# One order of steps for another: the merge of attention and MLP in seven of eight loops (RWKV-6 attention, then an exact-GELU MLP)

## The chip, the core and the metric

The kernel runs on one core of a Trainium2 chip. The metric is the device time of one execution in microseconds (us); lower is better.

## The reference

Attention is a linear recurrence over 768 positions, for 4 batches x 8 heads of 48 values; an MLP with the exact GELU follows on its output. All of it is fp32.

```python
for t in range(S):                       # S = 768
    kt, vt, rt, wt = (k[:, :, t], v[:, :, t], r[:, :, t], w[:, :, t])
    cur = np.einsum('bhd,bhe->bhde', u[None] * kt, vt)
    y[:, :, t] = np.einsum('bhd,bhde->bhe', rt, state + cur)
    state = wt[:, :, :, None] * state + np.einsum('bhd,bhe->bhde', kt, vt)
x = y.transpose(0, 2, 1, 3).reshape(3072, 384)
h = x @ w_in                             # 384 -> 2048
g = 0.5 * h * (1.0 + erf(h / sqrt(2)))
return g @ w_out                         # 2048 -> 384
```

## The kernel before

The 3072 tokens are cut into eight tiles of 384 (half a batch each). For each tile there are three generators of work, and a `yield` in them ends a *step*:

- `attention(x, unit)` works in chunks of 64 positions. DVE lays out the decayed r and k (L394, L401, L407, L427, L435, and L579 with ACT's L573 in `quarters`); PE multiplies them in small 64x64 matmuls, in bursts (`burst`, L595 and L604); DVE and ACT copy the results into the score tile `a_sb` (L637, L687 on DVE, L620 on ACT, where a later copy and the next burst on the same banks wait for each other). `blocks_of_k` transposes k on DVE (L552), and 12 DMAs on the SP queue (L547) move its blocks; L711 on ACT copies the rest (in the second tile PE's transposes L701 and ACT's L703 do this). Then come the matmuls into `kv_ps` (L727), a chain of 20 or so small DVE operations that carries the state from chunk to chunk (L742), the matmuls of scores by v into `y_ps` (L768, `inside`), two small DVE copies that read `y_ps` (L780, `fences`), and the matmuls of the state by r into the same `y_ps` (L813), which wait for the fences. ACT copies `y_ps` to `xT` (L836, L839), and DMAs move a part of it (L843).
- `mlp(x)` takes `xT`. *h passes* are the first product: L1070 for the first two tiles, L945 for the others (in halves, combined by sums so that fewer products are needed), with GELU on ACT (L1073, L1075, L977, L981). *o passes* are the second product: L1164 for the first tile, L1084 for the others, four or eight matmuls to a step; ACT and DVE take the results from PSUM (L1120 to L1207, among them L1181, L1203 and L1207 near the end of a tile).
- `load(x)` issues the DMAs of a tile's r, k, w and v on the SP queue (L192, L172). `sums_of_x` (L913 on DVE) prepares sums of `xT` for the MLP; it reads what the DMAs of L843 bring. In the second tile `w_sums` (L860) and in the third `first_sum` and `h_sums` make sums of the weights on DVE, and up to the second tile `conversion` turns fp64 weights into fp32 (L349, L350, L352 on ACT, L361 and L365 on DVE).

Loop `x` of eight merges the MLP of tile `x - 1`, the attention of tile `x`, the head of the attention of tile `x + 1` and the loads of tile `x + 1`. The merge is written out by hand: `PLAN[x]` is a string, and each of its characters takes one step of a stream:

```python
for c in PLAN[x]:
    next(streams[c], None)
```

The letters are `.` for `mlp(x - 1)`, `s` for `attention(x)`, `f` for the head of `attention(x + 1)`, `l` for the loads, `x` for `sums_of_x`, `w` for masks and sums of weights, `c` for the conversion. (In loop 0 they stand for other streams.) What a string leaves over is taken behind it, stream by stream. Behind the last loop `mlp(7)` runs alone.

The schedule is manual: instructions go to each engine's queue in the order in which the steps issue them, and each engine works through its queue in that order, waiting by semaphores for what an instruction needs. So a string decides what stands ahead of each instruction on PE, ACT, DVE and on SP's queue of DMAs. Loops are called 0 to 7 here; loop 1 makes the attention of the second tile. On PE the loops begin at 48.9 (loop 1), 124.4, 197.1, 261.3, 332.5, 396.7 and 467.9 us (loop 7), and `mlp(7)` at 532.4 us of the profiled execution.

Of the kernel before, what the change touches and what calls it, by code (L numbers as in the profile page):

```python
# [38 lines left out]
PLAN = {  # L39
    0: ".lls.....sslsc.lsslll.sl.sls..sl.lscsl..sss.lscs.lscs.s.clll.s..s.pcsss...wss..sccs.ffp",  # L40
    1: (
        ".cswc.ccc.cccss.lc.ccscs..cc.cs.cclwcsc.ccssc.c.cccsccc..ssccc.c.lcls.cc.ccsc.w.clwscclccc"
        ".c.swcw.ss.ccs.lcsc..cwcccslccslff..w..fw.wfs..f..flffffffww"
    ),
    2: (
        "...l...s..ws.swssswssss.sslsw...ssss.sssws.ll..ws.w..lw.sw.wl.sls.sls..lf.s....sf..f.f.xx."
        "fxl.x.x"
    ),
    3: (
        "l..sss..s.s..s.s....s...s.ssllss.sss.s.s.ss.l..lsss..ssslss.ss.s..s......s..ls.llssf.sf.sf"  # L50
        "lf.f.x.x..xxfffxf"
    ),
    4: (
        "...s...lsl......s.s....sss..ssss..s..ss..s..s...llssslss....sl.sss...s...sll.sl.s.sfs..fsf"
        ".ff..xl.x.xfffxffx"
    ),
    5: (
        ".l..........ls.ss...s.sslls.ssss..ss.sls...sss..sssssl.ss.s..s.......s.lssll.sfsf.f.s.ff.x"
        "..x.xxxl"
    ),  # L60
    6: (
        "sss.sls.....s......ls.s....s.sssssss..s.....s.ss....s.s.ssss.s.l.ss.l.ls.l...s.l.lslssf.s."
        ".ffs..lff.xx..xffxffx"
    ),
    7: "......s.s....s.s...s.ssssss...sss.ss...sss..ssss.s...ss...s...s.s.ss.s.s.s.x.x...xxx",
}


# [5 lines left out]
def kernel(  # L74
# [6 lines left out]
    w_out: bass.AP,  # L81
    out: bass.AP,
):

    nc = tc.nc  # L100
    NX = rkw.shape[0]
    NP = u.shape[1]
# [1227 lines left out]
```

## Time and the profile before

| | |
|---|---|
| three runs, us | 593.58, 595.18, 594.47; median 594.47 |
| profiled execution, first to last instruction | 595.7 us (1.2 above the median; nothing further is shown around it) |
| instructions | 17417 |
| PE busy | 578.9 us, 97%, 7536 matmuls |
| DVE busy | 440.2 us, 74% |
| ACT busy | 280.9 us, 47% |
| POOL busy | 8.0 us, 1% |
| DMA | 46.80 MB, mean 79 GB/s |

PE is TensorE's matmuls, DVE is VectorE, ACT is ScalarE, POOL is GpSimd, SP is SyncE, whose queue issues the DMAs. In the profile's lines `out<-in` names the tiles; `xN` is a number of instructions; a bracket holds the idle time of the engine ahead of an instruction and what ended it. In the table by stages each line has the stretch and its length, then the busy time of PE, PEld (weight loads), DVE, ACT and POOL, the clock granted to PE (1.00 is full speed), the share of DMA and the GB/s.

### The profile page before, as it was taken

To read this page: it belongs to the slowest core of one execution; us is meant where nothing else is said; L and a number is where in the kernel's file an instruction comes from. 1 tells how busy PE (TensorE), PEld (TensorE's weight loads), DVE (VectorE), ACT (ScalarE), POOL (GpSimd) and SP (SyncE) were. 2 spreads that over 40 slices of the span, in tenths; PEclk is the share of its full clock that TensorE was granted. 3 is DMA by queue.
4 is the path that set the end of the run, shared out by engine and by line. 5 is a ranking of instruction groups with operands and counts; after the bars stand their busy time and mean duration, and the time that the engine had idled before them with its cause. 6 is when DMAs were issued, how large, how long until landed. Compare 5 with 4: busy or idle time off the path is not lost. (4 is left out here: it accounts for less than half of the span.)

```text
span 595.7 us, 17417 instructions
## 1 busy us (share of the span) xinstructions
PE 578.9 (97%) x7536; PEld 513.5 (86%) x7536; DVE 440.2 (74%) x854; ACT 280.9 (47%) x648; POOL 8.0 (1%) x21
## 2 busy tenths in 40 slices
PE   5789999999999999999999999999999999999998
PEld 3566666676799999999999999999999999999997
DVE  5868767888969987687859987688759998521332
ACT  2158889333622358045561458135560465435400
POOL 3100000000000000000000000000000000000000
PEclk9989999999999999999999999999999999999999
DMA  7657671120152211241023411330015200210000
GB/s 235 193 175 273 211 237 61 71 94 1 19 148 79 74 54 24 74 137 36 1 52 90 124 37 18 96 110 11 3 32 161 72 2 5 37 46 0 1 15 33
DMA packets 51004, 46.80 MB, mean 79 GB/s; under 512 B 31728, under 2 KB 36080, under 8 KB 50928
## 3 DMA queue, kind: packets, MB, share of 16 engines
q1 hardware_dynamic: 50832, 45.62, 25.5%
q8 instruction: 59, 0.97, 0.7%
q14 instruction: 17, 0.14, 0.1%
q10 hardware_dynamic: 96, 0.07, 0.1%
HBM read 36.24 MB, written 4.72 MB: 69 GB/s over the span
## 5 line engine op out<-in xcount | busy, mean ns | idle before, releaser
L945 PE MATMUL h_ps<-xT,w_in_sb 128*128 128x192 f32 x480 | 95.4, 330 | 0.5 <-DVE o_sb L1207 0.5
L945 PEld LDWEIGHTS h_ps<-xT,w_in_sb 128*128 128x128 f32 x480 | 79.7, 190 | 3.9 <-ACT g L977 1.5
L1070 PE MATMUL h_ps<-xT,w_in_sb 128*128 128x384 f32 x192 | 64.5, 491 | 0.9 <-ACT rkw L1075 0.9
L1070 PEld LDWEIGHTS h_ps<-xT,w_in_sb 128*128 128x128 f32 x192 | 35.7, 190 | 25.5 <-ACT rkw L1075 1.7
L1084 PE MATMUL o_ps<-w_out_sb,g 128*128 128x192 f32 x224 | 39.7, 326 | 0.0
L1084 PEld LDWEIGHTS o_ps<-w_out_sb,g 128*128 128x128 f32 x224 | 37.0, 190 | 0.3
L945 PE MATMUL u_ps<-s,w_in_sb 128*128 128x192 f32 x192 | 35.3, 327 | 0.0
L468 PEld LDWEIGHTS d<-rkw 64*64 64x64 f32 x1152 | 20.8, 147 | 16.7 <-issue 11.9
L620 ACT COPY a_sb<-d 32x256 f32<-32x256 f32 (+8 forms) x90 | 32.6, 362 | 4.6 <-PE d L604 3.1
L945 PEld LDWEIGHTS u_ps<-s,w_in_sb 128*128 128x128 f32 x192 | 31.8, 190 | 0.2
L1084 PE MATMUL o_ps<-w_out_sb,f 128*128 128x192 f32 x176 | 31.6, 329 | 0.0
L1084 PE MATMUL o_ps<-t,g 128*128 128x192 f32 x176 | 31.4, 329 | 0.0
L1084 PE MATMUL o_ps<-w_out_sb,e 128*128 128x192 f32 x176 | 31.4, 329 | 0.0
L1084 PE MATMUL o_ps<-t,e 128*128 128x192 f32 x176 | 31.2, 328 | 0.0
L1084 PE MATMUL o_ps<-t,s 128*128 128x192 f32 x176 | 30.9, 327 | 0.0
L468 PE MATMUL d<-rkw 64*64 64x64 f32 (+1 forms) x1152 | 23.5, 235 | 7.2 <-DMA rkw<-in_rkw_dram 4.1
L742 DVE SCALAR_TENSOR_TENSOR st<-st,tot_sb,kv_ps 128x48 f32<-128x48 f32 x160 | 29.0, 256 | 1.7 <-PE kv_ps L727 1.6
L637 DVE COPY_PREDICATED a_sb<-quarter,d 128x480 f32<-128x480 uint8 (+5 forms) x54 | 23.2, 438 | 8.6 <-PE d L604 7.3
L1084 PEld LDWEIGHTS o_ps<-t,g 128*128 128x128 f32 x176 | 28.7, 190 | 0.4
L1084 PEld LDWEIGHTS o_ps<-w_out_sb,e 128*128 128x128 f32 x176 | 28.7, 190 | 0.3
L1084 PEld LDWEIGHTS o_ps<-w_out_sb,f 128*128 128x128 f32 x176 | 28.7, 190 | 0.3
L1084 PEld LDWEIGHTS o_ps<-t,e 128*128 128x128 f32 x176 | 28.8, 190 | 0.2
(163 smaller groups left out, 1127.0 us busy)
## 6 DMA issues: line engine op xcount, KB each, us to landing
rkw<-in_rkw_dram SPq DMA_DIRECT2D x54, 256.0 KB, 4.0
raw<-in_w_out_dram SPq DMA_DIRECT2D x8, 768.0 KB, 4.5
v_in<-in_v_dram SPq DMA_DIRECT2D x8, 584.0 KB, 3.9
raw<-in_w_in_dram SPq DMA_DIRECT2D x5, 768.0 KB, 6.5
out_dram<-o_sb SPq DMA_DIRECT2D x20, 192.0 KB, 2.0
rkw<-kx SPq DMA_DIRECT2D x72, 48.0 KB, 2.0
rkw<-in_rkw_dram SPq DMA_DIRECT2D x6, 384.0 KB, 6.8
raw<-in_w_in_dram SPq DMA_DIRECT2D x9, 256.0 KB, 4.7
```

The lines of the kernel that those rows point to most:

```text
L468: nc.tensor.matmul(d[half[p], g, n * width:(n + 1) * width], lhsT=kc[half[g], b, i, p], rhs=right(half[g], b, i, p), start=True, stop=True)
L620: nc.scalar.copy(out=at[z, g, first:behind, (a + 1) * h:], in_=d[z, :, :, to] if g == slice(None) else d[z, :, to])
L637: nc.vector.copy_predicated(out=an[:, :, :, :, (a + 1) * h:], mask=mask.to_broadcast(data.shape), data=data)
L742: nc.vector.scalar_tensor_tensor(out=stq[:, q, c], in0=stq[:, q, c - 1] if c else b4[:, q, NC - 1], scalar=totq[:, q, c:c + 1], in1=kvs[q ...
L945: nc.tensor.matmul(o, lhsT=lhsT, rhs=rhs, start=start, stop=True, skip_group_check=True)
L1070: nc.tensor.matmul(h_ps, lhsT=w_in_sb[:, f // FI, j, f % FI * 128:(f % FI + 1) * 128], rhs=xT[:, j, :], start=(j == 0), stop=(j == NJ - 1))
L1084: nc.tensor.matmul(o, lhsT=lhs(j), rhs=rhs(j), start=start and j == 0, stop=(j == HF - 1), skip_group_check=True)
```

## The change

The strings of loops 1 to 7 are replaced by others with the same steps in another order. Within each stream the order of steps stays as it was; between the streams it changes. Where a string holds fewer `f` than before, those steps of the head come in the next loop, as `s`. The string of loop 0 stays, as does all code that issues instructions. Sixteen blank lines at the head of the kernel go, so that a line's number is 16 lower afterwards (L813 becomes L797).

```diff
 PLAN = {
     0: ".lls.....sslsc.lsslll.sl.sls..sl.lscsl..sss.lscs.lscs.s.clll.s..s.pcsss...wss..sccs.ffp",
     1: (
-        ".cswc.ccc.cccss.lc.ccscs..cc.cs.cclwcsc.ccssc.c.cccsccc..ssccc.c.lcls.cc.ccsc.w.clwscclccc"
-        ".c.swcw.ss.ccs.lcsc..cwcccslccslff..w..fw.wfs..f..flffffffww"
+        "c.c.s.cs.ccc.csccscs.c.ccc.cccslcccss.sc.cl.sccccccs..l.wwcsc.c.cscccc.cs.c..sscwlc.cc.ccl"
+        "cswsccwccsccwcw.cl.csl.sccllf..c.ff...w.sffswwfwlw...."
     ),
     2: (
-        "...l...s..ws.swssswssss.sslsw...ssss.sssws.ll..ws.w..lw.sw.wl.sls.sls..lf.s....sf..f.f.xx."
-        "fxl.x.x"
+        "s.l.sss.lss.s..ss.ss.wwws.ss.w.lw.ss.lsssss.s.wsss.sssw.w..l.w...l.sws..ls.sls..l...fsfl.."
+        "sf.f..fx.xxxx"
     ),
     3: (
-        "l..sss..s.s..s.s....s...s.ssllss.sss.s.s.ss.l..lsss..ssslss.ss.s..s......s..ls.llssf.sf.sf"
-        "lf.f.x.x..xxfffxf"
+        "sll.ss.sss....s....s....ss.ssss..s..ssss.l.l.s.sss..ssss.sss.l........s.ssl.s.slsllslsf.f."
+        ".f.fxxxxx...f"
     ),
     4: (
-        "...s...lsl......s.s....sss..ssss..s..ss..s..s...llssslss....sl.sss...s...sll.sl.s.sfs..fsf"
-        ".ff..xl.x.xfffxffx"
+        "ls..s..s.sl...sls...s..s...sl.sssss..s..ss.lss..s.....s.ssl..s.ss..ss.s....s.s.ls.ss.llfs."
+        "ff.s..ff.l.xx.xfxx"
     ),
     5: (
-        ".l..........ls.ss...s.sslls.ssss..ss.sls...sss..sssssl.ss.s..s.......s.lssll.sfsf.f.s.ff.x"
-        "..x.xxxl"
+        "sls.s..sl..l...ss....sl.l..s.ssss.s.sss..s.ss...sss.sssss..s..s..l..s..s.slssls..lsfs..f.x"
+        "f.x.fx.x.fxl"
     ),
     6: (
-        "sss.sls.....s......ls.s....s.sssssss..s.....s.ss....s.s.ssss.s.l.ss.l.ls.l...s.l.lslssf.s."
-        ".ffs..lff.xx..xffxffx"
+        "l.ss.sss........s..lls.s..l.l.ss.lss.ss..s.ss...ss..s..s..s..s.ssss..ss.s....ssl..ls.slfsf"
+        "..fs.ffx..x..xxxl"
     ),
-    7: "......s.s....s.s...s.ssssss...sss.ss...sss..ssss.s...ss...s...s.s.ss.s.s.s.x.x...xxx",
+    7: "ss..s..s.....ss.s..s...s.sssssss...ss...s..ssss.sssss..s....s..s.s...ssss...ss....xxx.xx",
 }
```

## The prediction

> **What bounds the kernel now.** I read the busy times of the page first, then the table by stages (one stretch per loop), the list of what PE waited for, and the chain that ended last. The page:
> ```profile
> PE 578.9 (97%) x7536; PEld 513.5 (86%) x7536; DVE 440.2 (74%) x854; ACT 280.9 (47%) x648; POOL 8.0 (1%) x21
> ```
> PE is busy for 578.9 of 595.7 us. The stages, cut at the loops' starts on PE (after the span come PE, PEld, DVE, ACT, POOL, clock, DMA share, GB/s):
> ```profile
> 48.00:124.00 76.00, 75.09 (x1072) 49.81 (x1071) 59.02 (x93) 58.98 (x98) 0.00 (x0) 1.00 0.50 165
> 124.00:197.00 73.00, 73.00 (x788) 58.07 (x786) 63.71 (x121) 24.65 (x63) 0.00 (x0) 1.00 0.23 67
> ...
> 332.00:396.00 64.00, 63.67 (x832) 60.67 (x832) 52.44 (x98) 32.28 (x84) 0.00 (x0) 1.00 0.25 67
> 396.00:468.00 72.00, 71.63 (x871) 69.18 (x870) 58.28 (x111) 33.01 (x83) 0.00 (x0) 1.00 0.23 65
> ```
> PE fills each loop that the change touches (75.1 of 76, 73 of 73, 63.7 of 64, 71.6 of 72 us), the clock is full, and DVE has 9 to 17 us to spare in each of these four. So the time there is PE's work plus PE's stalls, and an order changes only these. The stalls:
> ```profile
> PE d L468 <- DMA rkw<-in_rkw_dram: 4.1, 1, 4.1
> PE d L468 <- issue: 2.3, 2, 1.8
> PE h_ps L1070 <- ACT rkw L1075: 0.9, 1, 0.9
> PE y_ps L768 <- DVE st L742: 0.7, 2, 0.4
> PE h_ps L945 <- DVE o_sb L1207: 0.5, 1, 0.5
> ```
> The first two are in the first tile, whose order stays. In the loops of the second to the eighth tile I count, from row to row of PE's timeline (start to start, which finds a little more than the list): 1.04 us (57.53, L1070 behind L1075), some 0.28 us twice at kv_ps (242.8 and 314.1, behind the DMAs of L547), 0.17, 0.27, 0.50 and 0.53 us at y_ps (behind the chain of states, L742), and 0.71 us at 468.4 (L945 behind L1207); together 3.8 us. That is all which a better order of the same work could win by stalls. The chain shows the last of them:
> ```profile
> 467.95 0.35 DVE o_sb L1203
> 468.30 0.28 DVE s L913
> 468.61 0.36 DVE xT L913
> 468.96 0.28 DVE o_sb L1207
> 469.29 2.22 PE h_ps L945 x12
> 471.51 0.65 PE u_ps L945 x4
> 472.16 2.15 PE h_ps L945 x12
> 474.30 1.30 PE u_ps L945 x8
> 475.60 1.95 PE h_ps L945 x12
> ```
>
> **What the change can win.** No instruction comes or goes; the steps of the streams are merged otherwise. Twelve h passes take 1.95 us in a row, and 2.15 us where they follow attention's 64x64 matmuls (last fence): a visit to these costs 0.2 us. I count the visits from the two strings, with the steps that hold matmuls: 9, 6, 7, 6, 7, 6, 7 in loops 1 to 7 before, and 8, 6, 6, 6, 6, 6, 6 after. Four fewer save 0.8 us. With the 3.8 us of stalls the ceiling of any gain is 4.6 us (0.8%). Issues of DMAs move on SP too: the loads of the next tile (4.0 us to landing) are awaited by DVE alone (0.5 us at L407 in loop 3 of before), which has time to spare; I put them at 0, and at 1 us if that spare time is gone (in the upper bound). The other DMAs are costed below.
>
> **What it can lose.** For each matmul that needs ACT or DVE, I took from the timeline how long its producer had been done (its slack), and added up what stands ahead of both in the new order, with the mean of each row. Where PE's work ahead shrinks more than the slack, or the producer's queue gets longer by more, PE waits. Differences to before, by loop:
>
> Loop 1. kv_ps (L727) comes 1.4 us of PE earlier, while the same ACT work stands ahead of its copies (a conversion L349, L350, L352 of 2.9 us, then L529, and L703 at 0.80 each). Its slack was 0.26 us, so it waits 1.1; I take 0.9, as PE already stands 0.4 us later by two waits behind L1075 (+0.3 and +0.1: a conversion is now queued ahead of them on ACT). The y_ps wait of 0.17 goes. In the string the last two "s" were parted by "." and are now parted by "ff", which is DVE work alone: the matmuls of L813 stand right behind those of L768 on PE, with only the fence between. Its latency shows at loop 7 of before:
> ```profile
> 521.21 1.63 PE L768 MATMUL y_ps<-a_sb,v_in 64*64 64x64 f32 x96
> 522.91 0.16 DVE L780 COPY fence<-y_ps 128x2 f32<-128x2 f32 x1 [0.45 <-PE y_ps L768]
> 524.26 1.63 PE L813 MATMUL y_ps<-rkw,st 64*64 64x64 f32 x96
> ```
> PE's next row began at 522.83, and the fence ended at 523.07, behind an idle DVE: 0.3 us with the signal back, which the o pass in between covered. With no pass between, it costs 0.3 (more if DVE is late). One visit less: -0.2. Sum: 0.9 + 0.4 - 0.17 + 0.3 - 0.2 = +1.2 us.
>
> Loop 1 into 2. L1181 frees the bank that the second h pass of L1070 needs; it had 1.75 us to spare. Its "." now comes after "wwfwlw", and DVE has behind the fence two of L427's (1.0), two of L401's steps with one L435 (2.2 and 2.5), four of L860 (0.95 each) and L1181 itself:
> ```profile
> 124.26 0.36 DVE L1181 TENSOR_TENSOR o_sb<-o_ps,rkw 128x192 f32<-128x192 f32 x1 [1.49 <-issue]
> ```
> That is 1.0 + 2.2 + 2.5 + 3.8 + 0.36 = 9.9 us, against 9.2 us of PE from the fence to that pass (L813 1.6, four o passes 5.3, the two of L131 0.4, the first h pass 1.9): +0.6. In before the same DVE had been idle here (1.49 us, the bracket). Attention's first d burst (L604) then waits 0.2 for L579, and kv_ps 0 to 0.5 for the DMAs of L547, issued 5 us later; I take 0.2. Sum: +1.0.
>
> Loop 3. The first burst arrives 1.4 us earlier against a slack of 1.23: +0.25. The kv_ps wait goes: -0.28. y_ps now follows L742's chain (20 x 0.2 us) with two o passes less between: +0.45. L768 and L813 are adjacent: +0.3. A visit less: -0.2. Sum +0.5.
>
> Loop 4. Two bursts wait for DVE, as a 2.2 us step of L401 is now behind the last L1181 in its queue: +0.45 and +0.2 against slacks of 1.19 and some 0.2. kv_ps gains 0.28 and y_ps gives as much back. Sum +0.65.
>
> Loop 5. One o pass less stands between two bursts that are chained by L620 on ACT (slack 0.41): +0.4. kv_ps behind L711 +0.15; adjacent L768 and L813 +0.3; visit -0.2; the first of L913 now waits in DVE's queue for the DMAs of L843 with L1181 behind it, and the second h pass waits for that: +0.45. Sum +1.1.
>
> Loop 6. First burst +0.4 (as in loop 4), the next behind L620 +0.35, the head of loop 7 (L945 behind L1200 and L1207, where the 0.71 is now) +0.3. Sum +1.05.
>
> Loop 7. A burst behind L620 +0.45, adjacency +0.3, visit -0.2: +0.55. The last MLP has no change.
>
> All taken in full: 1.2 + 1.0 + 0.5 + 0.65 + 1.1 + 1.05 + 0.55 = +6.0 us. But a wait also gives every later producer of the loop time. With only the largest of the DVE and ACT waits counted in each loop, and the fences, visits and vanished stalls as above, it is +0.8, +0.8, +0.3, +0.45, +0.55, +0.7 and +0.55, together +4.1. I take +5, between the two. The profiled execution (595.7 us from first to last instruction) is 1.2 us above the median of the runs, 594.47; the difference is taken over: 600.7 for an execution like the profiled one, **599.5** by the median. The bounds of the unknown terms: below, half of the counted waits are covered, +2; above, none is and DVE is late at the fences (0.5 more each) and for a load (1 us) too, 6 + 2 + 1 = +9. So 596.5 to 603.5 for this case alone.
>
> **Rivals.** *Faster, 591.6.* The waits that I count rest on slacks of 0.1 to 1.8 us and on row means; if ACT and DVE run ahead by some 1 us more at the kv_ps, L620 and L1181 points than I add up, none appears, and the visits (-0.8), kv_ps (-0.56), the y_ps of loop 1 (-0.17) and the 0.71 at the head of loop 7 with half of the other y_ps waits go: about -2.9. It decides at L1181 behind loop 1's L860s: if that pass does not wait, my tally is too dark everywhere. For it speaks DVE's 26% of idle time; against it the many slacks of under 0.5 us in the rows of before. *No change, 594.5.* The gains in my sums are 0.8 + 0.56 + 0.17 = 1.5 us, so the waits in them are 7.5; if a fifth of these comes true, it is even. *Slower by the clock, 602.* PE ran at half speed for 3.4 us after an idle piece of 1.8 us, in the first tile:
> ```profile
> 28.50:31.90 3.40, 3.40 (x86) 2.45 (x90) 2.29 (x6) 1.24 (x4) 0.00 (x0) 0.50 0.34 87
> ```
> The 1.04 us stall at 57.5 left the clock at 1.00 (first row of the stages). If two of my waits fall together, most likely kv_ps in loop 1 behind a late conversion, a stall of 1.8 us would cost 3.4 x 0.5 = 1.7 us more, and 0.8 for the longer wait: +7.5. The Trainium skill ("TensorE: Matmul & The Clock Gate", section "HAM oscillation — how this bites in real kernels") puts the limit for idle gaps at about 3.4 us; by it no wait here would touch the clock and this rival would fall away, but the trace shows the drop after 1.8 us, so the row decides. The same page (section "A second HAM failure mode: psum-queue depth-cycling") tells of frequent short idles that make the clock swing; the short stalls of loops 1 to 7 in before did not, by the 1.00 in all their rows.
>
> **How the numbers follow.** Main case 0.66, by the clock 0.08, no change 0.12, faster 0.14. The measurement can tell some 0.3%, 1.8 us, from no change: faster is under 592.7, slower over 596.3. The main case lies over that but for a tail of 0.04, which goes to "same": faster 0.14, same 0.12 + 0.04 = 0.16, slower 0.62 + 0.08 = 0.70. The range reaches up to 603.5, the main case's end and past the clock's 602, and down to 593.0, which takes in no change and leaves out most of the faster case.
>
> **What would show it.** Right: in the profile after, PE waits at L797 (now L813's number, as 16 blank lines go) behind L764 in loops 1, 3, 5 and 7 of 0.3 us each; at L711 behind L687 near 104 us of about 1 us; at L1054 behind L1165 in the second pass of loop 2 of 0.6 us; several at L588 behind L604 and L563. The same 7536 matmuls. Wrong: PE's idle time from 48 us on is not above the 3.8 us of before; or the clock is below 1.00 in these loops; or the loss sits in DMA waits, which I put at 0.2 us in all.

## The result and the profile after

The changed kernel takes 600.35 us (median of four runs, 599.31 to 601.78) against 594.83 us before (four runs, 593.58 to 595.20): a ratio of 1.0102 with a 95% interval of 1.0071 to 1.0134, or 5.5 us more. The forecast was 599.5 us.

The profiled executions differ less (597.5 against 595.7 us from first to last instruction). The first tile, whose string is the same, makes that: PE began the first h pass at 44.66 us after and at 48.85 us before. So all comparisons of profiles here run from that pass to the last matmul: 543.58 us before and 549.60 us after, **6.0 us more**. The order of the profiles' line numbers is that of each kernel's own file: L813 of before is L797 after.

The page of the profile after, the line of busy times:
```profile
PE 576.2 (96%) x7536; PEld 511.3 (86%) x7536; DVE 439.9 (74%) x854; ACT 280.7 (47%) x648; POOL 8.0 (1%) x21
```
The same instructions on every engine, and on PE 2.7 us less busy time in a longer span. The stages, with the starts that the loops have now (length, then PE, PEld, DVE, ACT, POOL, clock, DMA share, GB/s):
```profile
48.00:126.00 78.00, 75.39 (x1075) 50.43 (x1074) 63.75 (x94) 54.51 (x92) 0.00 (x0) 1.00 0.49 163
126.00:199.00 73.00, 71.83 (x790) 58.29 (x789) 58.41 (x117) 25.10 (x65) 0.00 (x0) 1.00 0.21 55
336.00:400.00 64.00, 63.18 (x826) 60.08 (x825) 49.56 (x96) 32.03 (x84) 0.00 (x0) 1.00 0.22 60
400.00:472.00 72.00, 71.44 (x870) 68.98 (x869) 60.25 (x115) 32.66 (x83) 0.00 (x0) 1.00 0.23 64
```
PE is idle for 2.6 us in the first stretch and 1.2 in the second, where before it was 0.9 and 0.0. The clock stays at 1.00. What PE waited for, the lines that bear on the loops of the change (total, times, longest):
```profile
...
PE kv_ps L711 <- ACT kx L687: 1.4, 2, 1.2
PE o_ps L1068 <- ACT ysb L823: 1.2, 1, 1.2
PE o_ps L1068 <- ACT p L1104: 1.2, 1, 1.2
PE y_ps L752 <- DVE st L726: 0.9, 3, 0.4
PE d L588 <- ACT a_sb L604: 0.8, 2, 0.4
...
PE y_ps L797 <- DVE fence L764: 0.5, 3, 0.2
...
PE h_ps L929 <- DVE o_sb L1191: 0.2, 1, 0.2
```
The first three of these are about 1.2 us each and new; the wait behind L1075 is gone; the one at the head of loop 7 (L1207, now L1191) fell from 0.5 to 0.2.

I then measured every gap between two matmuls' starts in PE's rows and took off the pace of that kind (163 ns for 128x192 columns, 323 for 128x384, 16 for the small ones, 0.1 us at a change between large and small), counting what exceeds it by over 0.18 us. From the first h pass on the excess is 3.61 us before and 10.63 after (+7.0). What is left when it is taken off, 539.97 and 538.97 us, fell by 1.0 us: the four visits fewer. By loop:

| loop | forecast | measured | what makes it (excess over the pace, us) |
|---|---|---|---|
| 1 | +1.2 | +1.55 | kv_ps behind L687 1.26, fence 0.37, behind L797 1.34; L1075's 1.04 gone |
| 2 | +1.0 | +1.43 | o pass behind L1104 1.33 |
| 3 | +0.5 | +0.20 | y_ps 0.34, fence 0.38 |
| 4 | +0.65 | +1.23 | burst behind L563 0.38, inside kv_ps 1.07 |
| 5 | +1.1 | +0.93 | burst behind L604 0.45, fence 0.26, y_ps 0.34 (0.40 before), behind L797 0.27 |
| 6 | +1.05 | -0.05 | y_ps 0.43, as before |
| 7 | +0.55 | +0.74 | burst behind L604 0.45, fence 0.37, inside L797 0.61, head 0.35 (0.71 before; the forecast has the head, +0.3, in loop 6) |
| sum | +6.0 | +6.0 | |

The sum agrees, the single loops do not all. Two of the reasons show in the timeline. Loop 1, where L752 and L797 now stand side by side:
```profile
112.27 0.16 DVE L764 COPY fence<-y_ps 128x2 f32<-128x2 f32 x1
112.73 0.30 PE L797 MATMUL y_ps<-rkw,st 64*64 64x64 f32 x4
112.98 0.16 DVE L764 COPY fence<-y_ps 128x2 f32<-128x2 f32 x1 [0.55 <-PE y_ps L752]
113.20 1.61 PE L797 MATMUL y_ps<-rkw,st 64*64 64x64 f32 x92 [0.17 <-DVE fence L764]
116.05 0.76 PE L1068 MATMUL o_ps<-w_out_sb,rkw 128*128 128x192 f32 x3 [1.24 <-ACT ysb L823]
```
Four matmuls of L797 run, the others wait for the second fence (start to start 0.39 us for a pace of 0.02). After the 92 there is a hole until 116.05 that was not in the forecast; the bracket puts it down to ACT's L823, which this product does not read. And loop 2:
```profile
161.11 3.28 ACT L604 COPY a_sb<-u_ps 32x128 f32<-32x128 f32 x12
...
164.41 0.32 ACT L1104 COPY p<-o_ps 128x192 f32<-128x192 f32 x1
...
164.78 0.92 PE L1068 MATMUL o_ps<-w_out_sb,g 128*128 128x192 f32 x4 [1.17 <-ACT p L1104]
```
L1104 frees the bank of the next o pass and stands on ACT behind twelve copies of attention, 3.28 us.

### The profile page after: what moved, and what is told of

The parts are those of the page before. It is cut to its first block, busy times and chain, and to the rows that moved or that the text cites. A ratio compares the mean times of both kernels' runs of the same rounds, so it can differ in the third digit from the quotient of the medians.

```text
span 597.5 us, 17420 instructions
## 1 busy us (share of the span) xinstructions
PE 576.2 (96%) x7536; PEld 511.3 (86%) x7536; DVE 439.9 (74%) x854; ACT 280.7 (47%) x648; POOL 8.0 (1%) x21
## 3 DMA queue, kind: packets, MB, share of 16 engines
HBM read 36.24 MB, written 4.72 MB: 69 GB/s over the span
## 4 chain that ended last, share of the span: by engine, by line
PE 83%; DVE 6%; ACT 5%; issue 3%; DMA 2%; SPq 1%; DVEq 0%; ACTq 0%
PE o_ps L1068 30%; PE h_ps L929 14%; PE u_ps L929 12%; PE h_ps L1054 11%; PE d L588 4%; PE d L452 2%; PE y_ps L752 2%; PE y_ps L797 2%; PE kv_ps L711 2%; PE o_ps L1148 2%; ACT a_sb L604 2%; DVE st L726 1%; DMA rkw<-in_rkw_dram 1%; DVE rkw L419 1%; DVE kx L385 1%
## 5 line engine op out<-in xcount | busy, mean ns | idle before, releaser
L1068 PE MATMUL o_ps<-w_out_sb,g 128*128 128x192 f32 x224 | 39.8, 327 | 1.2 <-ACT p L1104 1.2
L1068 PEld LDWEIGHTS o_ps<-w_out_sb,g 128*128 128x128 f32 x224 | 36.9, 190 | 1.7 <-ACT p L1104 1.5
L604 ACT COPY a_sb<-d 32x256 f32<-32x256 f32 (+8 forms) x90 | 32.6, 362 | 3.6 <-PE d L588 2.2
L1068 PE MATMUL o_ps<-w_out_sb,f 128*128 128x192 f32 x176 | 31.7, 330 | 0.0
L1068 PE MATMUL o_ps<-t,s 128*128 128x192 f32 x176 | 31.3, 329 | 0.1
L452 PEld LDWEIGHTS d<-rkw 64*64 64x64 f32 x1152 | 19.3, 137 | 13.8 <-issue 9.1
L1068 PE MATMUL o_ps<-t,e 128*128 128x192 f32 x176 | 31.0, 328 | 0.0
L1068 PE MATMUL o_ps<-t,g 128*128 128x192 f32 x176 | 30.8, 329 | 0.0
L1068 PE MATMUL o_ps<-w_out_sb,e 128*128 128x192 f32 x176 | 30.7, 327 | 0.0
L983 DVE TENSOR_TENSOR g<-g,o_sb 128x384 f32<-128x384 f32 x24 | 13.2, 548 | 22.1 <-ACT o_sb L965 22.1
L1068 PEld LDWEIGHTS o_ps<-t,s 128*128 128x128 f32 x176 | 28.8, 190 | 0.6 <-issue 0.4
L1068 PEld LDWEIGHTS o_ps<-w_out_sb,f 128*128 128x128 f32 x176 | 28.7, 190 | 0.4
L1068 PEld LDWEIGHTS o_ps<-t,g 128*128 128x128 f32 x176 | 28.7, 190 | 0.3
L1068 PEld LDWEIGHTS o_ps<-t,e 128*128 128x128 f32 x176 | 28.8, 190 | 0.2
L1068 PEld LDWEIGHTS o_ps<-w_out_sb,e 128*128 128x128 f32 x176 | 28.9, 190 | 0.1
```

The lines of the kernel that those rows point to most:

```text
L452: nc.tensor.matmul(d[half[p], g, n * width:(n + 1) * width], lhsT=kc[half[g], b, i, p], rhs=right(half[g], b, i, p), start=True, stop=True)
L604: nc.scalar.copy(out=at[z, g, first:behind, (a + 1) * h:], in_=d[z, :, :, to] if g == slice(None) else d[z, :, to])
L983: nc.vector.tensor_add(g_of(q, 0, 1), g_of(q, 0, 1), z)
L1068: nc.tensor.matmul(o, lhsT=lhs(j), rhs=rhs(j), start=start and j == 0, stop=(j == HF - 1), skip_group_check=True)
```

## The experiments

**Again.** The changed kernel without an edit, for a second profile.

> The changed kernel once more, nothing altered, for its profile. Gaps that come from semaphores (kv_ps in loop 1 1.26 us over the pace, L1068 behind L1104 1.33, the fences 0.37, 0.38, 0.26, 0.37, y_ps 0.34 to 0.43, the bursts behind L604 0.45) should recur within 0.1 us. If the gaps of 1.34, 0.27 and 0.61 us near L797 and the 1.07 us in kv_ps of loop 4 come from instruction fetches, they differ from the first profile by 0.3 us or more in at least one place, and each ends 1.2 to 1.6 us after the end of a fetch; if they come from semaphores they recur within 0.1 us.

599.82 us. The gaps by semaphore recurred: kv_ps 1.29, L1104 1.33, the fences 0.37, 0.37, 0.26, 0.37, the bursts behind L604 0.46 twice. The others did not all: behind L797 1.29 in loop 1, none in loop 5, 0.35 in loop 7, none inside kv_ps of loop 4 (there y_ps waits 0.44 instead). So more than one kind of gap is mixed here. From the first h pass to the last matmul this execution took 548.38 us, 4.8 more than before.

**Shift.** PE's instructions are brought from memory by transfers of 16 KB. The page of the profile after has 59 of them, for 15223 rows of matmuls, weight loads and sequencer instructions, some 258 each; a block is 256 below. This run has 192 instructions more at the head of PE's stream, so that its blocks are cut elsewhere in the work:

```diff
     keep_warm(8)
+    tiny = ps.tile([128, BANK], F32, name="warm", tag="mm", bufs=2)
+    for _ in range(96):
+        nc.tensor.matmul(tiny[:, 0:16], lhsT=zeros[:, 0:128], rhs=zeros[:, 0:16], start=True, stop=True)
```

> The changed kernel with 96 tiny matmuls (zeros, 16 columns) more at its very start, which adds 192 instructions to PE's stream ahead of everything; nothing else changes. The three gaps in question end at instructions 4289, 10945 and 14273 of PE's stream, all 193 beyond a multiple of 256. Theory B (instruction fetch): the boundary now falls 64 instructions later in the work, behind the dense stretch or in another place of it; the gaps move: in loop 1 the gap between L797 and L1068 is no more than 0.4 us, and where gaps of this kind occur they end again near 193 modulo 256. Theory A (ACT's L823 or another semaphore): gaps stay at the same matmuls, 1.46, 0.43 and 0.63 us within 0.15. The time is not compared (the start is changed).

Its one run took 599.27 us, which is not compared, since its start is another. The same place in loop 1, in the timeline of this run (L782 is L797, L1053 is L1068):
```profile
113.19 0.30 PE L782 MATMUL y_ps<-rkw,st 64*64 64x64 f32 x4
113.66 1.61 PE L782 MATMUL y_ps<-rkw,st 64*64 64x64 f32 x92 [0.17 <-DVE fence L749]
115.21 2.54 PE L1053 MATMUL o_ps<-w_out_sb,rkw 128*128 128x192 f32 x14
```
The fence's gap is where it was; the hole behind the product is gone (113.66 + 1.55 = 115.21), in loop 5 as well, and new holes stand inside L797 of loop 3 (1.02 us) and of loop 7 (1.08). Counted in PE's rows, with the 14 that this trace lacks added, they end at instructions 7616 and 14529, 192 and 193 beyond a multiple of 256: the same residue as the three holes near L797 in the first profile. ACT's order is the same in both runs, so a semaphore of ACT would have left the hole in its place. The trace's DMA records show a transfer (a *fetch*) on PE's instruction queue next to each hole:

| profile, place | fetch begins, takes | PE goes on | after the fetch's end |
|---|---|---|---|
| after, loop 1 | 112.88, 1.88 | 116.05 | 1.29 |
| after, loop 5 | 386.96, 0.88 | 389.34 | 1.50 |
| after, loop 7 | 524.09, 1.15 | 526.57 | 1.33 |
| again, loop 1 | 114.61, 1.75 | 117.73 | 1.37 |
| again, loop 7 | 524.83, 0.96 | 527.08 | 1.29 |
| shift, loop 3 | 248.59, 1.04 | 250.98 | 1.35 |
| shift, loop 7 | 524.22, 1.44 | 527.01 | 1.35 |

192 small matmuls with their weight loads are 384 instructions in some 3.2 us; a fetch brings 256, and from its start until PE has them take 2.2 to 3.2 us. Where L752 and L797 stand together, PE can run dry. The Trainium skill ("Runtime: NRT & Kernel Launch", section "Instruction fetch mechanics") has the blocks of 16 KB and 256 instructions, and calls the cost of crossing one "mostly hidden"; the blocks agree with this trace, and hidden is not what the seven rows above show, at 0.3 to 1.3 us of excess each.

The gap of 1.07 us inside kv_ps of loop 4 is of another kind, although it too ends 1.28 us behind a fetch (312.65 + 0.88, then 314.81). Its residue is 224, and it stands ahead of the seventh of L711's 96 matmuls. These wait for the 12 DMAs of L531 (L547 of before), and here one of them took 4.2 us, where the median is 2.0:
```profile
L531 SPq DMA_DIRECT2D rkw<-kx x12: 585/618/646, 303.1 to 310.5; - x12
...
DMA to landing us min/median/max: 2.0/2.0/4.2
```
It was the last, issued at 310.52; it landed at 314.72, and PE went on 0.09 us later. The seventh matmul goes on 0.09 us behind the last landing in four more profiles, that of before (314.33) and those of three runs told below: "ACT's queue" (317.18), "close in before" (317.10) and "mended" (311.97). In before and the last two, no fetch ends in the 3 us ahead of it. In "again" and "shift" the last landing came before these matmuls began, and no gap is there. So PE waited here for a late DMA. Why it was late no run shows; in "ACT's queue" too a fetch ends 1.28 us ahead, so a fetch may have held it up.

**Apart.** One o pass put back between L752 and L797 in loops 1, 3, 5 and 7:

```diff
-1: ....ff...w.sffswwfwlw....     3: ...slsllslsf.f..f...   5: ...lsfs..f.x...    7: ...ssss...ss....xxx.xx
+1: ....ff...ws.ffswwfwlw....     3: ...slsllsl.sff..f...   5: ...lsf.s.f.x...    7: ...ssss...s.s...xxx.xx
```

> The changed kernel with one o pass put back between the matmuls of L752 and those of L797 (y_ps) in loops 1, 3, 5 and 7. Theory A (fence alone): the four gaps of 0.27 to 0.39 us within L797 go, 1.2 us in all, and four visits more cost 0.8: 600.0, no change that can be measured; the 1.46 us gap behind L797 in loop 1 (which the list of waits puts down to ACT's L823), 0.43 us in loop 5 and 0.63 us in loop 7 stay. Theory B (192 small matmuls with their weight loads are 384 instructions in 3.1 us, more than PE's instruction fetches of 16 KB, 256 instructions each, can bring): those three gaps shrink below 0.3 us too, another 1.9 us, and of that some 0.6 comes back as the wait of the second h pass of loop 2 behind L1165, which the 1.46 us had covered: 598.7.

600.4 us (ratio to before 1.0095, 1.0058 to 1.0131): nothing gained, and the profile says why. All gaps in and behind L797 are gone: those of the fence, as both theories had it, and the holes, as theory B alone had it. In their place stand three of 0.83, 1.96 and 0.61 us at the heads of loops 4, 6 and of the last MLP, where theory B had one of 0.6 at another place. Loop 5 into 6 (L879 is L913 of before, L1147 is L1181, L911 is L945):
```profile
395.33 0.36 DVE L879 TENSOR_TENSOR s<-xT 128x192 f32<-128x192 f32 x1 [3.08 <-DMA xT<-ysb]
...
397.34 1.10 DVE L393 TENSOR_TENSOR tot_sb<-tot_sb 128x192 f32<-128x192 f32 x4
398.36 0.35 DVE L879 TENSOR_TENSOR s<-xT 128x192 f32<-128x192 f32 x1
398.74 0.36 DVE L879 TENSOR_TENSOR s<-xT,s 128x192 f32<-128x192 f32 x1
399.02 0.35 DVE L1147 TENSOR_TENSOR o_sb<-o_ps,rkw 128x192 f32<-128x192 f32 x1
...
399.42 0.76 PE L911 MATMUL h_ps<-xT,w_in_sb 128*128 128x192 f32 x3 [1.80 <-DVE o_sb L1147]
```
L797 came one pass later and with it the DMAs of xT; DVE stood 3.08 us at the first sum with 3.7 us of steps queued behind it, the last of them L1147, for which the h pass waits. In the changed kernel L797 comes a pass earlier, and this wait stays hidden.

**Apart, sums late.** As the last, and the sums of x (`x`) behind the last o pass in loops 3, 5 and 7:

```diff
-3: ...f.f..f.fxxxxx...f      5: ...lsf.s.f.xf.x.fx.x.fxl     7: ...s.s...xxx.xx
+3: ...f.f..f.f...xxxxxf      5: ...lsf.s.f.f..f..xxxxfxl     7: ...s.s....xxxxx
```

> The changed kernel with one o pass put back between L752 and L797 in loops 1, 3, 5 and 7, as in the run before, and with the sums of x (the x steps, L897) of loops 3, 5 and 7 moved behind the last o pass of the loop. In the run before, the second h pass of the next loop had waited 0.8, 2.0 and 0.6 us for L1165, which stood on DVE behind these sums, and DVE had waited 3.1 us at the first of them for the DMAs of xT in loop 5. Theory (a step that waits for a DMA at the head of DVE's queue holds L1165): these three waits fall below 0.3 us each, the gaps in and behind L797 stay away, and the time is 600.4 - 3.4 + 0.5 = 597.5. Rival (L1165 is late by DVE's work alone): the waits stay within 0.4 us, 600.4.

602.27 us (1.0139, 1.0116 to 1.0163). The expectation failed: the waits behind L1165 are gone, but each came back as 0.68 us behind the sums themselves (L897), which now come too late for the second h pass, and a burst in loop 4 waits 1.02 us where it had waited 0.43. Three waits of 3.4 us became 2.0 us, and other steps lost more than that.

**ACT's queue.** In loop 1 the transposes and copies of k ahead of one conversion, in loop 2 one step of L604 behind L1104's:

```diff
-1: ...clcswsccwccsccwcw...      2: ...wsss.sssw.w..l.w...
+1: ...clcswssccwccccwcw...      2: ...wsss.ssw.w.s.l.w...
```

> The changed kernel with two steps moved: in loop 1 the step of L685 and L687 (transposes and copies of k) goes ahead of one conversion (3.0 us of ACT), and in loop 2 one step of 12 copies of L604 (3.3 us of ACT) goes behind the step of L1104. Theory (ACT's queue order is the whole cause): kv_ps in loop 1 no longer waits (1.68 us gap to under 0.4), and the o pass behind L1104 (gap 1.49 us at 164.8) no longer waits; loops 1 and 2 together 2.4 to 2.6 us shorter, unless kv_ps in loop 2 (0.29 us of slack behind L695) takes up to 0.5 of it. Rival (the copies wait for PE and DVE, not for the queue): both gaps stay over 1 us.

602.0 us in its one run. Both gaps are at the pace, so ACT's order was their cause. But the conversion that was passed now feeds its weights late, as the list of waits shows (L1130 is L1164 of before, L331 is L365):
```profile
PE o_ps L1130 <- DVE w_out_sb L331: 1.2, 1, 1.2
```
The 1.26 us moved from kv_ps to an o pass at 111.3 us (1.32); the 1.33 behind L1104 did not come back. Loops 1 and 2 together became 0.9 us shorter, where 2.4 to 2.6 were expected. This execution also met holes of the fetch kind, 1.50 us in loop 1, 1.17 in loop 3, 0.46 and 0.90 in loops 5 and 7; PE goes on at the same instructions as in the table (residue 193), 1.25 to 1.58 us behind a fetch's end.

**Loops 1 and 2 as before.** The changed kernel with the two strings of before.

> The changed kernel with the two strings of loops 1 and 2 put back to those of before. From the two profiles, PE took 1.54 us more for loop 1 and 1.44 us more for loop 2 than before, and 3.05 us more for loops 3 to 7. Theory (the loss is a sum of separate waits, loop by loop, and one loop does not lean on another): 3.0 us above before, 597.8 by a median of 594.8 (ratio 1.005), and loops 3 to 7 keep their starts relative to each other within 0.3 us of the changed kernel's. Rival (the early loops shift DMAs and buffers for the later ones, so that the later loops lose only because the early ones were late): the time falls to before's, 595.

596.22 us (1.0026, 1.0001 to 1.0050), between the theory's 597.8 and the rival's 595. The gaps by semaphore in loops 3 to 7 are the same as in the changed kernel (fences 0.37, 0.26, 0.37; bursts 0.39, 0.46, 0.46; y_ps 0.34 and more), so they do not hang on the early loops. What is missing are the holes of the fetch kind (0.27 + 0.61 us in the changed kernel's first profile) and the late DMA (1.07); y_ps of loop 4 waits 0.43 instead, as in "again". 3.05 - 1.95 + 0.43 = 1.5 us; from the first h pass on this profile is 1.4 us longer than before's, and the times say 1.6.

**Close in before.** The kernel before with L768's step moved down to L813's in the same four loops, the change's adjacency alone:

```diff
-1: ...cslccslff..w..fw.wfs..f...   3: ...llssf.sf.sf   5: ...lssll.sfsf.f.s.ff.x   7: ...s.ss.s.s.s.x.x...xxx
+1: ...cslcclff..w..fw.wfss..f...   3: ...llssf.f.ssf   5: ...lssll.sff.f.ss.ff.x   7: ...s.ss.s..ss.x.x...xxx
```

> The kernel before with one part of the change alone: in loops 1, 3, 5 and 7 the step of L768 (y_ps) is moved down to stand directly ahead of the step of L813, nothing else. Theory (fence and instruction fetch): a gap of 0.25 to 0.40 us within L813 in each of the four loops, 1.4 us in all; beside it gaps of 0.3 to 1.5 us that end 1.2 to 1.6 us after the end of an instruction fetch, in some of the four loops (none in at least one); less 0.8 us for four visits and up to 0.4 us for y_ps in loop 5, which no longer waits for L742: 0.5 to 3 us slower, about 596. Rival (the gaps of the changed kernel come from its other steps): no gap over 0.2 us within L813, 0.8 to 1.2 us faster.

606.0 us (1.0199, 1.0183 to 1.0216), far beyond the expectation. The fences move with L768, and here DVE has other steps queued ahead of them. Loop 5:
```profile
389.21 1.63 PE L768 MATMUL y_ps<-a_sb,v_in 64*64 64x64 f32 x96
390.25 1.78 DVE L394 TRANSPOSE_TENSOR_REDUCE rkw<-kx 128x48 f32<-128x1536 f32 x1
...
394.37 0.22 DVE L780 COPY fence<-y_ps 128x2 f32<-128x2 f32 x2
394.58 0.61 PEld L813 LDWEIGHTS y_ps<-rkw,st 64*64 64x64 f32 x18 [3.87 <-DVE fence L780]
394.58 0.69 PE L813 MATMUL y_ps<-rkw,st 64*64 64x64 f32 x14 [3.74 <-DVE fence L780]
```
L813 waited 3.95, 1.44 and 3.94 us in loops 1, 3 and 5, and 0.38 in loop 7, where nothing stood on DVE ahead of the fences. So the gap of 0.25 to 0.40 us that was expected in four loops came in one: 0.26 to 0.38 us is the price of adjacency with DVE at hand, and in the changed kernel DVE was at hand in all four loops. No hole of the fetch kind shows in this execution. The long waits also show when the clock falls, in the stretches behind the gaps of 3.97 and 3.96 us (columns as in the stages above; the clock is the third figure from the end):
```profile
117.57:121.00 3.43, 3.43 (x99) 3.31 (x100) 2.13 (x2) 0.49 (x2) 0.00 (x0) 0.53 0.00 0
394.58:398.00 3.42, 3.42 (x100) 3.35 (x101) 0.01 (x1) 0.49 (x2) 0.00 (x0) 0.61 0.02 5
```
and behind the 2.12 us gap of the run "apart":
```profile
399.42:402.80 3.38, 3.38 (x19) 3.15 (x20) 3.35 (x4) 1.39 (x3) 0.00 (x0) 1.00 0.64 176
```
In the first tile less was enough. There the clock of before fell a second time, at 42.1 us, behind one gap of 1.89 us:
```profile
41.34 0.20 PE L727 MATMUL kv_ps<-v_in,kx 64*64 64x48 f32 x1 [1.89 <-issue]
...
42.00:43.70 1.70, 1.70 (x53) 1.70 (x46) 1.70 (x11) 0.00 (x0) 0.00 (x0) 0.54 0.28 62
43.70:45.40 1.70, 1.70 (x40) 1.70 (x39) 1.09 (x5) 0.48 (x1) 0.00 (x0) 0.50 0.79 300
```
Five more profiles ("again", "loops 1 and 2 as before", "sums late", "close in before", "mended") show a fall at 38 to 41 us behind a gap of 2.0 to 2.6 us; the changed kernel's first profile has 2.55 us near that place, and "apart" 2.0, without one.

**Mended.** The kernel before, with its own waits taken on.

```diff
-4: ...sl.s.sfs..fsf.ff...    5: ...lssll.sfsf.f.s.ff.x...    6: ...lslssf.s..ffs..lff.xx..xffx...
+4: ...sl.s.sf.s.fsf.ff...    5: ...lssll.sff.sf.s.ff.x...    6: ...lslssf..s.ffs..lf.xx..fxffx...
```

> The kernel before with its own waits in loops 4 to 6 taken on: the step of L768 goes behind the next o pass in loops 4, 5 and 6 (it waited 0.25, 0.40 and 0.43 us for L742 there), and one 2.2 us step of L401 in loop 6 goes behind the step of L1207 (for which the second h pass of loop 7 waited 0.71 us). Theory (these waits are the whole of it, and the fences keep an o pass between L768 and L813): 1.3 us faster, 593.3, ratio 0.998. Rival (L407 stands on DVE ahead of the fences, so that L813 waits for them as long as L768 did, and the delayed sums give back the rest): no change, within 0.4 us.

597.79 us (1.0066, 1.0043 to 1.0089): slower, nearer to the rival and worse than it. The waits at y_ps went, but in loop 5 the fences came to stand behind L394 and L813 waited 2.13 us; the moved step of L401 made a burst of loop 7 wait 1.38 us for L579; and kv_ps of loop 4 waited 1.4 us for late DMAs of L547.

**Mended, with DVE's backlog left alone.** In loop 1 a conversion behind the second h pass, in loop 4 L768 as above, in loop 6 two sums of x behind L1207:

```diff
-1: .cswc.ccc.cccss...    4: ...s.sfs..fsf...    6: ....ffs..lff.xx..xffxffx
+1: .csw.cccc.cccss...    4: ...s.sf.s.fsf...    6: ....ffs..lff...xxxffxffx
```

> The kernel before with three waits of its own taken on, each in a way that leaves DVE's backlog as it is: in loop 1 a conversion (3.0 us of ACT) goes behind the second h pass, whose L1075 the fourth h pass waited for (1.0 us); in loop 4 the step of L768 goes behind the next o pass (0.25 us); in loop 6 two of the sums of x (L913) go behind the step of L1207 (0.6 us of the 0.71 at the head of loop 7). Theory (each wait stands alone): all three below 0.3 us, 1.8 us faster, 592.6, ratio 0.997. Rival (ACT is the bound of loop 1, by its chain of conversions up to the copies of L703): the 1.0 us comes back as a wait of kv_ps behind L703 in loop 1 or of L1164 behind a conversion; 0.8 us faster, ratio 0.9985, which cannot be told from no change.

595.27 us (1.0009, 0.9989 to 1.0029), no change. The list of waits from the second tile on:
```profile
PE kv_ps L727 <- DMA rkw<-kx: 0.8, 1, 0.8
PE h_ps L945 <- DVE xT L913: 0.7, 1, 0.7
PE y_ps L768 <- DVE st L742: 0.7, 2, 0.4
PE h_ps L1070 <- ACT rkw L1075: 0.2, 1, 0.2
```
Of the 1.04 us behind L1075, 0.37 is left (0.2 in the list, which had 0.9), and it did not come back as the rival had it; the head of loop 7 only changed its cause (0.71 behind L1207 to 0.89 behind L913), and kv_ps of loop 4 shows 1.04 us (0.8 in the list, behind DMAs), which is 0.2 in before. No version here beats the kernel before.

## Why the prediction was right, and where it was not

Time and direction held: +5 us forecast, +5.5 by the medians, +6.0 and +4.8 by two profiles. Step by step, in the prediction's own order:

- **Visits**, -0.8: -1.0 us in PE's time net of gaps, in both profiles.
- **kv_ps in loop 1**, +0.9 (bound 1.1): 1.26 and 1.29. The deduction for earlier waits behind L1075 was wrong: these were forecast at 0.4 more, and instead the 1.04 us of before went away too. The new string starts with other conversions ahead of the second h pass; I had taken the old wait as unchanged.
- **Fences**, 4 x 0.3: 0.37, 0.38, 0.26, 0.37, and "apart" takes away all four. Right, on the condition that DVE is idle there, which the prediction has only as "more if DVE is late" and as 0.5 in the upper bound; "close in before" shows it to be worth up to 3.9 us.
- **L1181 at the head of loop 2**, +0.6: no wait, and not only because the hole behind L797 gave DVE time, for the shifted run has no hole there and no wait either. The step that failed is the DVE sum: 9.9 us by the rows' durations, where the shifted run took 9.2 us from the fence (113.61) to the end of this L1181 (122.78), since DVE's rows overlap by some 0.1 us at each join. Summed durations are too long by that; the starts are what count. The rival "faster" had named this pass as its sign that the tally is too dark everywhere. Too dark it was, by the terms of the next point that did not come.
- **Bursts and y_ps**: the 0.4 and 0.45 us at L604 in loops 5 and 7 came as 0.45 and 0.45, the first burst of loop 4 as 0.38 (0.45), y_ps of loop 3 as 0.34 (0.45), kv_ps in loop 5 as 0.14 (0.15). Those of loops 3 and 6 (0.25, 0.4, 0.35), the second burst of loop 4 (0.2) and the sums in loop 5 (0.45) did not come, nor did the small waits at the head of attention in loop 2 (0.2 twice) and the 0.3 more at the head of loop 7, where 0.36 less was measured; the wait behind the sums is real, as "apart" shows with 1.96 us, but the early L797 covers it. Of the gains, kv_ps of loop 3 was to lose its 0.28 us and kept 0.2.
- **Not in the forecast**: L1104 behind L604 on ACT in loop 2, 1.33 us. I followed what attention waits for and passed over the o passes' own copies on ACT. Then the instruction fetches, 2.2 us in one execution and 1.6 in the other. And in the first profile the late DMA at kv_ps of loop 4, 1.07 us, where the prediction had a gain of 0.28 and 0.2 us of DMA waits in all.
- **The rival by the clock**: no clock fell in the loops, and no gap there reached the 1.8 us that this rival asked for (the longest is 1.68 us from start to start, at kv_ps). How long a gap must be is not settled. In the loops of the other runs gaps of 2.12 and 2.40 us left the clock at 1.00, and gaps of 3.97 and 3.96 us brought it to half for 3.4 us; in the first tile 1.89 us was enough, once. The Trainium skill ("TensorE: Matmul & The Clock Gate", section "HAM oscillation — how this bites in real kernels") gives about 3.4 us; the loops agree with that and the first tile does not. So the row that the prediction read was right for its place, but it could not be carried over to the loops. What tells the two places apart stays open. The place of a gap in time may count too: in each profile the clock's changes lie on a grid of 3.41 us ("close in before": 38.86, 117.37 and 393.85 us, 23 and 81 steps apart), and the gaps of 2.40 and 2.55 us that left the clock alone are cut in two by this grid, at 386.96 and 36.24 us.

So the sum is right with a part of luck: terms of 4.0 us came as 4.4, terms of 3.6 us did not come, and 1.3 us by L1104, 1.6 to 2.2 us by fetches and in one profile 1.1 us by a late DMA stood in for them. That the total held rests on the ground that was common to all: PE was full, there were 3.8 us to win, and a new order meets many slacks below 0.5 us.

## What to carry to other kernels

Where one engine is full and the others feed it by queues, a merge of the same work is judged by slacks: list every producer with under 1 us to spare, from both sides (the bank that the next product needs counts like its operands), and sum DVE and ACT work from start to start. A wait that is taken away by moving a step often comes back at the next step with little slack, as five edits here showed, though not always: 1.3 us behind L1104 and 0.7 behind L1075 stayed away. Before two dense stretches of small matmuls are put side by side, ask what lay between them: an o pass there hid a fence and an instruction fetch, and pushed back a transfer.

## What the runs showed of the hardware

- PE's instructions come in blocks of 256 (16 KB). 384 instructions in a row at 8 ns each ran PE dry by 0.3 to 1.5 us, not in each execution; in eleven such holes of four profiles PE went on 1.25 to 1.6 us after a transfer ended. The list of waits names another engine or "issue" for it.
- A gap that ends 1.28 us behind such a transfer can still be another's: at kv_ps of loop 4, PE went on 0.09 us behind a DMA's landing, in five profiles.
- In the loops the granted clock fell to half, for some 3.4 us, behind idle gaps of 3.96 and 3.97 us, and stayed at 1.00 behind gaps of 2.12 and 2.40 us. In the first tile, from 25 us on, it fell in six of eleven profiles, behind gaps of 1.8 to 2.6 us. Its changes lie on a grid of 3.41 us.
